# Attention opening of a three-stage kernel: gates of all chunks made together, factor products on another engine, factor set-up in three pieces

## The chip, the cores and the metric

One core of a Trainium2 chip runs the whole program. The metric is the device time of one execution in microseconds. The kernel before took 759.8 us, the median of three runs (759.53 to 760.16).

## What is computed

Three stages follow one another: a gated linear attention with a running state, a mixture of eight experts with one expert for each token, and a dense MLP. The change is in the first. For each batch entry and head it computes, token after token:

```python
m_new = maximum(f_gate[t] + m, i_gate[t])
f_stab = exp(f_gate[t] + m - m_new)
i_stab = exp(i_gate[t] - m_new)
C = f_stab * C + i_stab * outer(v[t], k[t])
n = f_stab * n + i_stab * k[t]
h = C @ q[t]
y[t] = sigmoid(o_gate[t]) * h / maximum(abs(n @ q[t]), 1)
```

There are 4 batch entries, 8 heads, 768 tokens and a head size of 40, all in float32.

## The kernel before

**Tiling.** The 768 tokens are six chunks of 128. A unit is one batch entry of one chunk with all its eight heads; units run chunk by chunk, so units 0 to 3 are chunk 0, units 4 to 7 chunk 1, and there are 24. For a unit, `scores_mm` (L470) multiplies keys with queries (16 products in PSUM), `scan` makes the matrix of decays between the unit's tokens, `scores_w` (L475) weights the scores with it, `pv` (L533) multiplies by the values, `state` (L484) makes the unit's part of the running state, which `state_up` (L501, L505) takes out of PSUM, `inter` (L520) is the part that comes from earlier chunks, and `epilogue1`, `epilogue2` (L545 to L561) and `finish` (L568, L571) normalise. `kweigh` (L461) and `vprime` (L454) weight keys and values on GpSimd. The rows of chunk 0's units are then turned and multiplied with the experts' embeddings (`route_t` L577, `route_l` L608).

**Gates.** The 32 pairs of batch entry and head lie in 32 partitions with the 768 tokens along the row. `fg` and `ig` hold three copies of these rows (96 partitions), loaded by six DMAs (L159): the first copy on SP's queue, the two others on ScalarE's. `gates_m` (L295) is the scan that gives the running maximum, `gates_x` (L300, L301) and `gates_xi` (L305, on VectorE for chunk 0 and on GpSimd for the others) the sums, `gates_exp` (L309) the exponentials. `gates_z` (L315, L316, L318, L319) sets the starts of the scans to zero and, for chunk 0, fills `f0`. `gates_e` (L323) scans the products of the decays.

**Two ways to the decay matrix.** For chunk 0, `scan0` broadcasts the decays of each head to all partitions with products (L445) and scans them on VectorE (L447), twice four heads for each unit. For later chunks the decays go to DRAM (`put_dec`, L276), come back broadcast (`fload`, L285, two DMAs a unit), are scanned over 64 tokens only (L423), and the block between the two halves of the chunk is one product (`far_mm`, L432) of two factors. The early factor `fa` is made by six doublings (`suffix`, L348: widths 63, 62, 60, 56, 48 and 32 for each of five chunks), then `factor_a` (L352, L354) and `spread_a` (L366, four ScalarE operations); the late factor `fb` by `factors` (L359, L361, L362) and `spread_b` (L370, eight ScalarE operations). `gates_pe` (L382 to L389) turns the gates for the later chunks and copies them out of PSUM.

**Order.** The whole attention stands in a manual schedule: each engine runs its instructions in the order of the program text, and each queue its DMAs. Before the loop the order is: loads of unit 0, gates of chunk 0, loads of units 1 and 2, unit 0's scan and scores. In the loop over units: the gates of the later chunks are scanned in unit 0 and finished in unit 1; `gates_z`, `put_dec` and `fload(4)` come in unit 2; the first three doublings in unit 2 and the last three in unit 3; `gates_e` and all of `spread_b` at the end of unit 2; `gates_pe` in unit 3; `factor_a`, `spread_a` and `far_mm(4)` at the end of unit 3. Every unit ends with the loads of the unit three ahead. Set-up that stands outside the manual schedule (constants, `ident_h` L202, masks) is put between by the scheduler.

Of the kernel before, what the change touches and what calls it, by code (L numbers as in the profile page):

```python
# [9 lines left out]
F32 = mybir.dt.float32  # L10
# [4 lines left out]
ALU = mybir.AluOpType  # L15
# [11 lines left out]
def kernel(ctx, tc, qT_in, kT_in, kvo_in, i_gate, f_gate, expert_emb, tau, w12, wio, out, dbg=None):  # L27
# [113 lines left out]
    with ExitStack() as actx:  # L141
# [15 lines left out]
        def load_gates(a, eng):  # L157
            for t, g in ((fg, f_gate), (ig, i_gate)):
                eng.dma_start(out=t[a * BH:(a + 1) * BH], in_=g.rearrange("b h s -> (b h) s"))  # L159

        load_gates(0, nc.sync)
        for a in range(1, 3):
            load_gates(a, nc.scalar)
# [125 lines left out]
        def rows_of(c0, c1, r=None):  # L289
            r = r or slice(0, R3 if c0 else BH)  # L290
            return (lambda t, o=0: t[r, c0 * P + o:c1 * P + o])
# [29 lines left out]
        def gates_e(c0, c1):  # L321
# [3 lines left out]
            n = c1 - c0  # L325
            factors()
            gd = wk.tile([BH, n, B * G], F32, tag="gd", name="gd", bufs=1)
            gd_t[c0] = gd
            nc.vector.tensor_tensor(out=gd, in0=pairm.unsqueeze(1).to_broadcast([BH, n, B * G]),
                                    in1=est[0:BH, c0:c1, P - 1:P].to_broadcast([BH, n, B * G]), op=ALU.mult)  # L330
# [10 lines left out]
        def suffix(second):  # L341

            if not second:
                nc.gpsimd.memset(facA[:, :, HP - 1:HP], 1.0)
                nc.gpsimd.tensor_copy(facA[:, :, 0:HP - 1], fz[:, CH:NCH, 1:HP])
            k = 8 if second else 1
            while k < (HP if second else 8):
                nc.vector.tensor_tensor(out=facA[:, :, 0:HP - k], in0=facA[:, :, 0:HP - k], in1=facA[:, :, k:HP], op=ALU.mult)  # L348
                k *= 2
# [6 lines left out]
        def factors():  # L356
# [5 lines left out]
            nc.vector.tensor_tensor(out=late, in0=late, in1=est[:, CH:NCH, HP - 1:HP].to_broadcast([R3, NCH - CH, HP]), op=ALU.mult)  # L362

# [500 lines left out]
        with tc.manual_schedule():  # L864
# [8 lines left out]
            gates_z(0, 1)  # L873
            nc.sync.dma_start(out=emb, in_=expert_emb)
# [12 lines left out]
            gates_pe0()  # L887
            scores_w(0)
# [3 lines left out]
            for u in range(0, NU - 1):  # L892
# [4 lines left out]
                if ok(u + 2) and u != 2:  # L897
                    fload(u + 2)
# [8 lines left out]
                if u == 1:  # L907
# [3 lines left out]
                    gates_x(1, NCH)  # L911
                    gates_xi(1, NCH)
                    gates_exp(fg, 1, NCH)
                    gates_exp(ig, 1, NCH)
                if u in (2, 3):
                    scores_w(u)
                if u == 2:
# [789 lines left out]
```

## Time and profile before

| | |
|---|---|
| median of three runs | 759.8 us |
| profiled execution | 758.68 us |
| its span on the core | 757.0 us |
| granted TensorE clock, mean | 0.987 |
| busy: TensorE, VectorE, ScalarE, GpSimd | 719.1, 518.7, 370.5, 228.0 us |
| attention units | to about 182 us of the span |

A span starts with the first instruction on the core; the execution's own time has 1.7 us more around it. PE is TensorE's products, PEld its weight loads, DVE VectorE, ACT ScalarE, POOL GpSimd, SP the engine whose queue issues most loads; a q behind the name is the engine's queue. PEclk is the granted clock, 1.00 for 2.4 GHz and 0.50 for 1.2 GHz. In a timeline a row stands for instructions merged (x3: three), with the start, the length, and in brackets how long the engine had been idle before it and what ended that.

### The profile page before, as it was taken

To read this page: it belongs to the slowest core of one execution; us is meant where nothing else is said; L and a number is where in the kernel's file an instruction comes from. 1 tells how busy PE (TensorE), PEld (TensorE's weight loads), DVE (VectorE), ACT (ScalarE), POOL (GpSimd) and SP (SyncE) were. 2 spreads that over 40 slices of the span, in tenths; PEclk is the share of its full clock that TensorE was granted. 3 is DMA by queue.
4 is the path that set the end of the run, shared out by engine and by line. 5 is a ranking of instruction groups with operands and counts; after the bars stand their busy time and mean duration, and the time that the engine had idled before them with its cause. 6 is when DMAs were issued, how large, how long until landed. Compare 5 with 4: busy or idle time off the path is not lost.

```text
span 757.0 us, 13429 instructions
## 1 busy us (share of the span) xinstructions
PE 719.1 (95%) x4773; PEld 674.9 (89%) x4773; DVE 518.7 (69%) x1090; ACT 370.5 (49%) x857; POOL 228.0 (30%) x349
## 2 busy tenths in 40 slices
PE   7679999998889999999999999999999999999995
PEld 7669988998788999999998888998889988899994
DVE  7957879897399989899976764544544554445542
ACT  4375455544466666676645443333333343334442
POOL 5434467785243333454401003003003003002011
PEclk9969999999999999999999999999999999999998
DMA  7258887772458766877832121201110201101000
GB/s 213 83 175 271 273 262 231 215 227 74 148 206 238 237 192 194 227 212 229 250 84 80 27 58 45 57 17 42 37 42 35 42 22 36 43 0 46 12 19 18
DMA packets 70106, 93.14 MB, mean 123 GB/s; under 512 B 31858, under 2 KB 56530, under 8 KB 70034
## 3 DMA queue, kind: packets, MB, share of 16 engines
q1 hardware_dynamic: 66770, 83.96, 38.2%
q0 software_dynamic: 3072, 7.89, 3.0%
q8 instruction: 38, 0.62, 0.3%
q10 hardware_dynamic: 192, 0.39, 0.2%
q14 instruction: 34, 0.28, 0.1%
HBM read 71.11 MB, written 17.18 MB: 117 GB/s over the span
## 4 chain that ended last, share of the span: by engine, by line
issue 42%; PE 23%; POOL 5%; DVE 2%; DMA 1%; ACT 0%; POOLq 0%; SPq 0%; ACTq 0%
PE acc L1207 12%; PE hp L138 10%; POOL out_dram L1252 3%; POOL xr L1358 2%; PE xt L1131 1%; DMA xr<-y 1%; DVE w L121 0%; POOL gap L1254 0%; DVE hs L1181 0%; DVE xl L1133 0%; DVE w L111 0%; DVE fr L1276 0%; POOLq L1702 0%; DVE xl L1149 0%; ACT hs L1520 0%
## 5 line engine op out<-in xcount | busy, mean ns | idle before, releaser
L1207 PE MATMUL acc<-wout,hhl 128*128 128x320 f32 x1152 | 187.0, 309 | 0.0
L1207 PEld LDWEIGHTS acc<-wout,hhl 128*128 128x128 f32 x1152 | 175.9, 188 | 7.4
L1192 DVE TENSOR_TENSOR sg<-hp,sg 128x512 f32<-128x512 f32 (+1 forms) x112 | 68.8, 614 | 93.3 <-ACT sg L1191 86.9
L138 PE MATMUL hp<-xh,win 128*128 128x512 f32 (+1 forms) x560 | 131.0, 364 | 0.0
L1191 ACT ACTIVATE sg<-hp 128x512 f32<-128x512 f32 (+1 forms) x112 | 60.3, 539 | 124.8 <-PE hp L138 124.2
L1194 DVE TENSOR_TENSOR hhl<-sg,hhl 128x512 fp32r<-128x512 f32 (+1 forms) x112 | 71.3, 636 | 70.2 <-ACT hhl L1193 70.2
L1252 POOL DMA_INDIRECT out_dram<-o,tokd x24 | 24.0, 1000 | 312.2 <-ACT o L1236 308.5
L1207 PE MATMUL acc<-w,hs 128*128 128x320 f32 x636 | 104.7, 310 | 2.0 <-ACT hs L1180 1.0
L138 PEld LDWEIGHTS hp<-xh,win 128*128 128x128 f32 x560 | 93.9, 188 | 11.5 <-ACT xh L1397 0.2
L1193 ACT CAST hhl<-sg 128x512 fp32r<-128x512 f32 (+1 forms) x112 | 62.6, 559 | 80.0 <-DVE sg L1192 76.5
L1207 PEld LDWEIGHTS acc<-w,hs 128*128 128x128 f32 x636 | 96.8, 188 | 4.2 <-DVE hs L1181 1.7
L138 PE MATMUL hp<-xl,win 128*128 128x512 f32 (+1 forms) x336 | 85.7, 363 | 0.0
L110 POOL TENSOR_TENSOR w<-r,w 128x256 fp32r<-128x256 f32 x58 | 47.3, 817 | 106.5 <-ACT w L105 83.9
L138 PEld LDWEIGHTS hp<-xl,win 128*128 128x128 f32 x336 | 58.8, 189 | 10.9 <-DVE xl L1398 0.2
L138 PE MATMUL hp<-xh,w 128*128 128x440 f32 (+6 forms) x320 | 66.8, 338 | 0.0
L138 PEld LDWEIGHTS hp<-xh,w 128*128 128x128 f32 x320 | 51.4, 189 | 1.7
L1180 ACT ACTIVATE hs<-hp 128x440 fp32r<-128x440 f32 (+6 forms) x64 | 30.2, 472 | 42.2 <-PE hp L138 38.0
L470 PE MATMUL sp<-qT,kblk 120*128 120x128 f32 x384 | 48.4, 281 | 1.3 <-DVE wm L475 1.3
L470 PEld LDWEIGHTS sp<-qT,kblk 120*128 120x128 f32 x384 | 46.5, 197 | 2.0 <-DVE wm L475 1.4
L533 PE MATMUL op<-vp_in,wm 128*128 128x96 f32 (+1 forms) x368 | 43.6, 272 | 0.0
L533 PEld LDWEIGHTS op<-vp_in,wm 128*128 128x128 f32 x368 | 42.9, 192 | 0.0
L138 PE MATMUL hp<-xl,w 128*128 128x440 f32 (+6 forms) x192 | 42.9, 331 | 0.0
(325 smaller groups left out, 1129.6 us busy)
## 6 DMA issues: line engine op xcount, KB each, us to landing
r<-in_w_dram SPq DMA_DIRECT2D x32, 704.0 KB
kvo<-in_kvo_dram SPq DMA_DIRECT2D x24, 480.0 KB
c<-in_wio_dram SPq DMA_DIRECT2D x16, 704.0 KB
fb<-dec SPq DMA_DIRECT2D x40, 128.0 KB
rows<-zt SPq DMA_DIRECT2D x8, 640.0 KB
qT<-in_qT_dram SPq DMA_DIRECT2D x24, 180.0 KB
xr<-y SPq DMA_DIRECT2D x5, 640.0 KB
kblk<-in_kT_dram SPq DMA_DIRECT2D x48, 60.0 KB
```

The lines of the kernel that those rows point to most:

```text
L110: eng.tensor_tensor(out=t[:, 3 * P:5 * P].rearrange("p (c f) -> p c f", c=2), in0=r1[:, 0:2], in1=hif[:, 0:2], op=ALU.subtract)
L138: nc.tensor.matmul(hp, a, b, start=(i == 0), stop=(i == len(seq) - 1))
L470: nc.tensor.matmul(sp[:, h - hs.start], kblk[u % NLD][0:KR, h // 3, h % 3, :], qT[u][0:KR, h // 3, :], start=True, stop=True)
L533: nc.tensor.matmul(ops[:, h * NW:h * NW + n], wm[u][:, h], vp_in[u % NLD][:, h * DV:h * DV + n], start=True, stop=True)
L1180: nc.scalar.activation(out=hh, in_=hp, func=AF.Relu)
L1191: nc.scalar.activation(out=sg, in_=hp, func=AF.Sigmoid, scale=1.702)
L1192: nc.vector.tensor_tensor(out=g, in0=hp, in1=sg, op=ALU.mult)
L1193: nc.scalar.copy(hh, g)
L1194: nc.vector.tensor_tensor(out=hl, in0=g, in1=hh.bitcast(F32), op=ALU.subtract)
L1207: nc.tensor.matmul(acc_t[blk][i], hl if j == 2 else hh, w[:, DM:2 * DM] if j == 1 else w[:, 0:DM], start=(first and j == 0), stop=(last an ...
L1252: sc = nc.gpsimd.indirect_dma_start(out=out, out_offset=bass.IndirectOffsetOnAxis(ap=tokd[:, ti:ti + 1], axis=0), in_=o[:, i], in_offset=None)
L1358: eng.tensor_tensor(out=xr_t[blk], in0=xr_t[blk], in1=gated[:, t0:t0 + n].unsqueeze(2).to_broadcast([P, n, 3 * P]), op=ALU.mult)
```

## The change

The scan, sums and exponentials of chunks 1 to 5 and the masks move ahead of unit 0's first scan; the scan of chunk 0 now takes all 96 rows at once, and the six gate loads are issued gate by gate instead of copy by copy. `gates_z`, `put_dec` and the decay loads of units 4 and 5 move ahead of unit 0's weighting, and so ahead of the loads of unit 3 on SP's queue. All six doublings go to GpSimd at the end of unit 0, with `gates_e` on VectorE; the late factors (`factor_b`) and half of `spread_b` come at the end of unit 1, `gates_pe` in unit 2, the other half of `spread_b`, `factor_a` and `spread_a` at the end of unit 2, and `far_mm(4)` at its common place in unit 3.

```diff
-        load_gates(0, nc.sync)
-        for a in range(1, 3):
-            load_gates(a, nc.scalar)
+        for t, g in ((fg, f_gate), (ig, i_gate)):
+            nc.sync.dma_start(out=t[0:BH], in_=g.rearrange("b h s -> (b h) s"))
+            for a in range(1, 3):
+                nc.scalar.dma_start(out=t[a * BH:(a + 1) * BH], in_=g.rearrange("b h s -> (b h) s"))
...
-            r = r or slice(0, R3 if c0 else BH)
+            r = r or slice(0, R3)
...
-            factors()
-            gd = wk.tile([BH, n, B * G], F32, tag="gd", name="gd", bufs=1)
...
-        def suffix(second):
-
-            if not second:
-                nc.gpsimd.memset(facA[:, :, HP - 1:HP], 1.0)
-                nc.gpsimd.tensor_copy(facA[:, :, 0:HP - 1], fz[:, CH:NCH, 1:HP])
-            k = 8 if second else 1
-            while k < (HP if second else 8):
-                nc.vector.tensor_tensor(out=facA[:, :, 0:HP - k], in0=facA[:, :, 0:HP - k], in1=facA[:, :, k:HP], op=ALU.mult)
+        def suffix():
+
+            nc.gpsimd.memset(facA[:, :, HP - 1:HP], 1.0)
+            nc.gpsimd.tensor_copy(facA[:, :, 0:HP - 1], fz[:, CH:NCH, 1:HP])
+            k = 1
+            while k < HP:
+                nc.gpsimd.tensor_tensor(out=facA[:, :, 0:HP - k], in0=facA[:, :, 0:HP - k], in1=facA[:, :, k:HP], op=ALU.mult)
                 k *= 2
...
-        def factors():
+        def factor_b():
...
             nc.vector.tensor_tensor(out=late, in0=late, in1=est[:, CH:NCH, HP - 1:HP].to_broadcast([R3, NCH - CH, HP]), op=ALU.mult)
+            n = NCH - CH
+            gd = wk.tile([BH, n, B * G], F32, tag="gd", name="gd", bufs=1)
...
             gates_z(0, 1)
+            gates_m(1, NCH)
+            gates_x(1, NCH)
+            gates_xi(1, NCH)
+            gates_exp(fg, 1, NCH)
+            gates_exp(ig, 1, NCH)
+            masks()
             nc.sync.dma_start(out=emb, in_=expert_emb)
...
             gates_pe0()
+            gates_z(1, NCH)
+            put_dec()
+            fload(4)
+            fload(5)
             scores_w(0)
...
-                if ok(u + 2) and u != 2:
+                if ok(u + 2) and u > 3:
                     fload(u + 2)
...
-                    gates_x(1, NCH)
-                    gates_xi(1, NCH)
-                    gates_exp(fg, 1, NCH)
-                    gates_exp(ig, 1, NCH)
...
-                if u == 2:
-                    gates_z(1, NCH)
-                    put_dec()
-                    fload(4)
...
-                    for a in range(1, 3):
-                        gates_m(0, 1, slice(a * BH, (a + 1) * BH))
-                    gates_m(1, NCH)
-                    masks()
...
-                if u in (2, 3):
-                    suffix(u == 3)
-                if u == 3:
+                if u == 2:
                     gates_pe(1, NCH)
...
-                if ok(u + 1) and u != 3:
+                if ok(u + 1):
                     far_mm(u + 1)
...
+                if u == 0:
+                    suffix()
+                    gates_e(1, NCH)
+                if u == 1:
+                    factor_b()
+                    spread_b(0, H // 2)
                 if u == 2:
-                    gates_e(1, NCH)
-                    spread_b(0, H)
-                if u == 3:
+                    spread_b(H // 2, H)
                     factor_a()
                     spread_a()
-                    far_mm(4)
```

## Rows read from the trace of the kernel before

**Rows 1.** Table of stretches: busy us of each engine, PEclk, DMA share, GB/s
```profile
20.00:33.00 13.00, 10.56 (x92) 10.07 (x92) 12.76 (x20) 4.83 (x11) 5.14 (x8) 1.00 0.18 55
33.00:52.00 19.00, 10.67 (x57) 9.35 (x56) 12.59 (x18) 11.98 (x33) 6.89 (x12) 0.64 0.64 201
52.00:70.00 18.00, 18.00 (x163) 17.72 (x163) 11.48 (x30) 10.63 (x35) 9.61 (x19) 1.00 0.68 206
...
230.00:757.00 527.00, 517.56 (x3133) 483.17 (x3131) 337.81 (x622) 250.85 (x517) 104.56 (x149) 0.99 0.32 91
```

**Rows 2.** Timeline of TensorE (start us, us, what, idle before)
```profile
7.04 3.78 PE L445 MATMUL f<-f,ident 128*128 128x128 f32 x16 [1.70 <-DVE f L319]
...
38.95 0.31 PE L383 MATMUL pg<-ident,fd 32*128 32x32 f32 x1 [4.78 <-DVE fd L362]
...
48.94 3.28 PE L470 MATMUL sp<-qT,kblk 120*128 120x128 f32 x16
...
56.26 1.95 PE L470 MATMUL sp<-qT,kblk 120*128 120x128 f32 x16
```

**Rows 3.** Timeline of VectorE
```profile
4.67 0.41 DVE L295 TENSOR_TENSOR_SCAN mm<-fg,ig 32x128 f32<-32x128 f32 x1 [0.89 <-DMA ig<-in_i_gate_dram]
...
18.57 0.86 DVE L295 TENSOR_TENSOR_SCAN mm<-fg,ig 32x128 f32<-32x128 f32 x2
...
22.45 1.32 DVE L300 TENSOR_TENSOR fg<-fg,mm 96x640 f32<-96x640 f32 x1
23.81 0.82 DVE L301 TENSOR_TENSOR fg<-fg,mm 96x640 f32<-96x640 f32 x1
...
32.61 2.75 DVE L348 TENSOR_TENSOR mm<-mm 96x315 f32<-96x315 f32 x3
35.28 2.08 DVE L323 TENSOR_TENSOR_SCAN fd<-fg,fd 96x640 f32<-96x640 f32 x1
37.89 0.48 DVE L361 TENSOR_TENSOR fb<-fd,fb 32x320 fp32r<-32x320 f32 x1 [0.53 <-ACT fb L359]
...
40.20 1.21 DVE L423 TENSOR_TENSOR_SCAN tri<-fb,id 128x512 f32<-128x512 f32 x1
43.71 0.17 DVE L557 SCALAR_TENSOR_TENSOR dn<-num 128x8 f32<-128x8 f32 x1 [2.30 <-ACT num L554]
...
44.24 2.56 DVE L348 TENSOR_TENSOR mm<-mm 96x280 f32<-96x280 f32 x3
...
52.33 1.22 DVE L475 TENSOR_TENSOR wm<-sp,pmb 128x1024 f32<-128x1024 f32 x1 [3.26 <-PE sp L470]
```

**Rows 4.** Timeline of the DMA issues and of ScalarE in the first 10 us
```profile
4.59 0.35 ACTq L159 DMA_DIRECT2D ig<-in_i_gate_dram  x1
...
5.91 0.29 SPq L874 DMA_DIRECT2D emb<-in_emb_dram  x1
...
9.39 0.47 ACT L404 ACTIVATE emb_sq<-emb 8x320 f32<-8x320 f32 x1 [3.14 <-DMA emb<-in_emb_dram]
```

**Rows 5.** Waits of SP's queue, 0 to 200 us (us in total, times, longest)
```profile
SPq L285 <- DMA dec<-fg: 2.4, 1, 2.4
```

**Rows 6.** Timeline of GpSimd
```profile
21.10 1.31 POOL L305 TENSOR_TENSOR ig<-ig,mm 96x640 f32<-96x640 f32 x1 [2.98 <-DVE mm L295]
22.38 0.72 POOL L454 TENSOR_TENSOR vp_in<-kvo,ei_tok 128x320 f32<-128x320 f32 x1
```

**Rows 7.** VectorE's groups by line and form, 0 to 60 us
```profile
L447 DVE TENSOR_TENSOR_SCAN pmb<-f,ident_h 128x512 f32<-128x512 f32 x8 | 9.4, 1209 | 1.5 <-PE f L445 1.5
```

**Rows 8.** Timeline of ScalarE
```profile
26.46 1.28 ACT L539 ACT_TABLE_LOAD   x1
...
38.41 3.73 ACT L370 ACTIVATE rhsB<-fb,hmask 96x320 fp32r<-96x320 f32 x8 [0.55 <-DVE fb L361]
...
47.84 1.92 ACT L366 ACTIVATE lhsA<-fa,bmask 96x320 fp32r<-96x320 f32 x4 [0.55 <-DVE fa L354]
```

**Rows 9.** Decay loads of SP's queue (ns min/median/max of one issue, first and last start)
```profile
L285 SPq DMA_DIRECT2D fb<-dec x40: 302/582/1857, 32.1 to 162.8; - x40
```

More of the change, by code (lines that the diff above doesn't have):

```diff
@@ L155 @@
         fg = ap1.tile([R3, S], F32, name="fg")
-        def load_gates(a, eng):
-            for t, g in ((fg, f_gate), (ig, i_gate)):
-                eng.dma_start(out=t[a * BH:(a + 1) * BH], in_=g.rearrange("b h s -> (b h) s"))
-        load_gates(0, nc.sync)
-        for a in range(1, 3):
-            load_gates(a, nc.scalar)
+        for t, g in ((fg, f_gate), (ig, i_gate)):
+            nc.sync.dma_start(out=t[0:BH], in_=g.rearrange("b h s -> (b h) s"))
+            for a in range(1, 3):
+                nc.scalar.dma_start(out=t[a * BH:(a + 1) * BH], in_=g.rearrange("b h s -> (b h) s"))
         NLD = 3
@@ L324, in gates_e @@
                                          op0=ALU.mult, op1=ALU.add)
-            n = c1 - c0
-            factors()
-            gd = wk.tile([BH, n, B * G], F32, tag="gd", name="gd", bufs=1)
-            gd_t[c0] = gd
-            nc.vector.tensor_tensor(out=gd, in0=pairm.unsqueeze(1).to_broadcast([BH, n, B * G]),
-                                    in1=est[0:BH, c0:c1, P - 1:P].to_broadcast([BH, n, B * G]), op=ALU.mult)
         def masks():
@@ L362, in factors @@
             nc.vector.tensor_tensor(out=late, in0=late, in1=est[:, CH:NCH, HP - 1:HP].to_broadcast([R3, NCH - CH, HP]), op=ALU.mult)
+            n = NCH - CH
+            gd = wk.tile([BH, n, B * G], F32, tag="gd", name="gd", bufs=1)
+            gd_t[CH] = gd
+            nc.vector.tensor_tensor(out=gd, in0=pairm.unsqueeze(1).to_broadcast([BH, n, B * G]),
+                                    in1=est[0:BH, CH:NCH, P - 1:P].to_broadcast([BH, n, B * G]), op=ALU.mult)
         def spread_a():
```

## The prediction, made before the changed kernel was run

> **What bounds the kernel now.** I read the table of stretches first, then TensorE's order of time, then those of VectorE, GpSimd and ScalarE, and last the queues. From 230 us on TensorE is busy 517.56 of 527 us, and from 52 to 70 us all 18.00 of 18 [rows 1]: there the products are the bound, and neither DMA nor another engine can win anything. The opening is different. From 20 to 33 us VectorE is busy 12.76 of 13 us and TensorE 10.56; from 33 to 52 us TensorE has only 10.67 of 19 us and its granted clock averages 0.64 [rows 1]. So the opening is set by VectorE, then by ScalarE and VectorE in turn, and TensorE pays twice. It stands idle 4.78 us until the late factors are made (L362), and after that it runs at the lower of its two levels, 1.2 instead of 2.4 GHz: the scores of unit 4 take 3.28 us for 16 products, those of unit 5 take 1.95 [rows 2]. What the change saves before unit 4 is weighted should stay saved, as all behind it is one train of products whose loads are issued unit by unit.
>
> **Where the end is measured.** I follow VectorE, because its list is fixed and nearly full, to the weighting of unit 4's scores (L475), which starts at 52.33 us [rows 3]. Two points lie on the way: the start of the first gate scan (4.67) and the end of unit 4's scan (40.20 + 1.21 = 41.41) [rows 3].
>
> **Part 1, the first gates wait for six loads.** Until now the first scan works on 32 rows and waits for SP's two loads. It will work on 96 rows, at the same length per row, so its own time stays, but it needs the loads on ScalarE's queue too, and the last of them goes out at 4.59 us [rows 4]; the new order of the loads leaves that one last. When it lands no row shows. Lower end: no later than SP's own, so the scan stays at 4.67. Upper end: the small embedding load is issued at 5.91 and its reader starts at 9.39, 3.48 us on [rows 4], which gives 8.07. The write of the decays is waited for 2.4 us past its issue of 0.35 or so, as that of ScalarE's load here [rows 4, 5], which gives 7.3. I take 7.7, between the last two: **+3.0 us**.
>
> **Part 2, moved gate work.** The scan over chunks 1 to 5, its two sums (1.32 and 0.82 us [rows 3]), GpSimd's subtraction (1.31 [rows 6]) and the two masks go ahead of unit 0's first scan. VectorE pays the same there as it paid later, so the chain only changes order. What lies behind them gets later (unit 0's scan, and all of unit 0), what lay behind them gets earlier. Two gains come with it: the two extra short scans for rows 32 to 95 go (**-0.86** [rows 3]), and VectorE's waits for the broadcast products, 1.5 us in eight scans [rows 7], are filled by the moved work (**-1.5**). The set-up from ident_h on stands behind the first gates now; I leave it there. ScalarE's exponentials all come before its other functions, so a return to their table goes, and with it the reload of the sigmoid's, 1.28 us [rows 8]; ScalarE has idle time around it, so I count nothing. Without that idle time it would be a gain of 1.28 for each.
>
> **Part 3, the doublings go to GpSimd.** VectorE loses 2.75 us before unit 4's scan and 2.56 us after it [rows 3]. GpSimd's two-input operations cost 0.72 us at 320 elements and 1.31 at 640 [rows 6], or 1.8 ns an element: widths 315, 310, 300, 280, 240 and 160 make about 3.8 us. They start behind unit 1's weighted keys; behind them wait v' and weighted keys of unit 2, which the products of unit 2 need a good 8 us later, and ScalarE's cast of the early factors, later still. So they lie beside other work: **-2.75** in the first stretch, nothing added. Without that cover every further us would come back as a us.
>
> **Part 4, ports.** While GpSimd made a v' of 0.72 us from 22.38 on, the 96x640 sum on VectorE (from 22.45) took 1.32 us, and its twin behind it 0.82 [rows 3, 6]: the loss is 0.5 us. The decay scan (2.08 [rows 3]) already had a GpSimd operation beside it and keeps its price. The Trainium skill (SBUF — State Buffer, Who interferes with whom) says that a VectorE operation with two SBUF inputs and a GpSimd operation that reads SBUF exclude each other, the later one blocking for the whole of the other; that speaks against this change, and the pair above agrees with it in kind. By the rule taken to its end the sum would be 2.6 us instead of 6.4, as a rival below has it.
>
> **Part 5, the factors in pieces.** The subtraction that ends the early factors (L354) moves ahead of unit 4's scan. Its price is 0.48 us, that of the same operation on the late ones (L361 [rows 3]); before it stands a wait for ScalarE's cast, which follows half of the head spreads (half of 3.73 [rows 8]). That wait lies between nothing and 1.9; I take 0.7 as ScalarE starts the half early: **+1.2** together. To the end of unit 4's scan: 41.41 + 3.0 - 0.86 - 1.5 - 2.75 + 1.2 = **40.5 us**.
>
> **Part 6, from there to unit 4's weighting** took 10.92 us before: 2.30 of wait for a copy that stood behind the spreads on ScalarE, the three doublings 2.56, unit 5's scan, a wait of 3.26 for slow scores, the rest small operations [rows 3]. Now ScalarE has half of the head spreads, a cast and the four batch spreads (1.92 [rows 8]) in front of unit 2's state copy, and this copy, the copy of unit 4's scan and that of unit 2's sums follow it. Walking these in order gives VectorE waits of 1.5 (sums), 1.6 (routing logits) and 0.4 (scores), with 1.2 for unit 5's scan and 0.7 of small work: **5.4 us**. That puts the weighting at 45.9 instead of 52.33: **6.4 us** earlier. In this walk TensorE's longest pause is 2.5 us, so I keep the full clock and the scores at 1.95.
>
> **Part 7, SP's queue.** The write of the decays and two units' decay loads now stand before the loads of unit 3. SP waits for the gates (about 18 us), 2.4 us for the write, and issues four loads at 0.58 [rows 9]: unit 3's loads start near 23 us and, with 3.48 to land, are there by about 29; its scores are due near 34. Counted as nothing; every us of lateness beyond 5 would cost one.
>
> **The sum.** The profiled execution took 758.68 us with a span of 757.0, the median of the three runs is 759.8, or 1.1 more. 758.68 - 6.4 = 752.3 there, and 759.8 - 6.4 = **753.4 us** against the median.
>
> **The rivals.**
> A. The sixth load lands with the first two, or nearly. For it: its queue had nothing else to do. Against: the issue at 4.59. It gives back 3.0: 750.4, and 749.2 if the waits of 0.7 (part 5) and 0.5 (part 4) do not come. Chance 0.16.
> B. The clock falls again in unit 3's pause, since 2.5 us idle, little work and 1.4 us idle follow each other. For it: 4.78 us of pause ended at half clock [rows 2]. The price is 3.28 - 1.95 = 1.33 for the scores and 0.8 for what surrounds them: 755.5. Chance 0.13.
> C. GpSimd's doublings shut VectorE out one by one, 3.8 us: 757.2. For it the pair of sums; against it, most of VectorE's work beside them reads PSUM, whose scans keep a mean of 1.21 us [rows 7]. Chance 0.04.
> D. The gain is made and lost again behind unit 4, or the lead is never there: 759.8, 0.05. Loads by unit and a full TensorE speak against it.
> E. Slower: TensorE starts cold and stays at the lower level. The pause before the broadcast products grows from 1.70 to 4.7 us, and they took 3.78 us for 16 even before [rows 2]. If the level stayed low through the work that now fills 20 to 33 us, its 10.56 us of products would take 21.1, 8.1 more than that stretch: the 6.4 lost and 1.7 on top, 761.5. It decides once more than some 8 us of products run at half speed beyond what VectorE covers. Against it: from 20 to 33 us the clock holds 1.00 although TensorE works only 10.56 of 13 us [rows 1]. Chance 0.06.
>
> **The numbers.** The forecast has 0.56. A measurement here can tell 0.2% (1.5 us) from no change. Faster: forecast, A, B and C, 0.89; same: D, 0.05; slower: E, 0.06. The range runs from A's 749.2 to C's 757.2, and leaves out D, E and little more.
>
> **What would show it.** Right: the first gate scan near 7.7 us; no idle TensorE before the gate transposes; six GpSimd products of 0.4 to 0.9 us by about 28 us; unit 4's weighting near 46; granted clock 1.00 from 33 to 52. Wrong: a gate scan past 10, a clock of 0.5 about the scores of unit 4, GpSimd operations over 1.5 us, or a pause of VectorE on a decay load.

## The result and the profile after

The changed kernel takes **752.12 us**, median of four runs (751.23 to 752.44), against 759.98 for the kernel before in the same comparison: a ratio of 0.9894, 95% interval 0.9877 to 0.9911. The prediction was 753.4. The profiled execution took 751.84 us with a span of 750.1 (before 758.68 and 757.0), so 6.8 us less. (With a fourth run, made beside the changed kernel's, the median of the kernel before is 759.98 instead of 759.8. In the ratios further down, four slow executions of 769 to 1432 us are left out: two of the kernel before, one of experiment 1 and one of experiment 7.)

The table of stretches of the changed kernel, against [rows 1]:

```profile
20.00:33.00 13.00, 11.99 (x109) 11.52 (x107) 12.73 (x19) 4.34 (x14) 8.62 (x12) 1.00 0.67 204
33.00:52.00 19.00, 17.37 (x137) 16.71 (x138) 12.48 (x23) 14.01 (x45) 13.07 (x24) 0.91 0.62 194
52.00:70.00 18.00, 17.15 (x157) 16.62 (x157) 13.42 (x38) 10.98 (x34) 8.74 (x11) 1.00 0.86 267
230.00:750.00 520.00, 510.69 (x3091) 476.68 (x3089) 330.90 (x609) 246.65 (x508) 100.93 (x144) 0.99 0.32 88
```

From 33 to 52 us TensorE went from 10.67 to 17.37 busy us, and its mean clock from 0.64 to 0.91: the pause and most of the half speed are gone. From 230 us on it is as full as before.

TensorE's timeline after, against [rows 2] (L440 is L445 of before, L465 is L470, L378 is L383):

```profile
10.32 3.39 PE L440 MATMUL f<-f,ident 128*128 128x128 f32 x16 [4.98 <-DVE f L316]
...
31.43 0.24 PE L378 MATMUL pg<-ident,fd 32*128 32x32 f32 x1 [0.36 <-DVE fd L352]
...
33.71 1.42 PE L479 MATMUL dC<-vp_in,kw 128*120 128x123 f32 x6 [1.30 <-ACT Cst L496]
34.92 3.01 PE L465 MATMUL sp<-qT,kblk 120*128 120x128 f32 x16
...
43.17 1.95 PE L465 MATMUL sp<-qT,kblk 120*128 120x128 f32 x16
...
49.16 1.95 PE L465 MATMUL sp<-qT,kblk 120*128 120x128 f32 x16
```

The pause of 4.78 us ahead of the gate transposes is 0.36 now. Up to unit 5 the clock still falls once, at unit 3: its scores take 3.01 us. Those of units 4 and 5 run at full speed, and unit 5's start at 49.16 instead of 56.26, 7.1 us earlier.

VectorE's timeline after, against [rows 3] (L292 is L295, L298 is L301, L320 is L323, L351 is L361, L344 is L354, L418 is L423, L470 is L475), and then GpSimd's, against [rows 6]:

```profile
8.04 0.42 DVE L292 TENSOR_TENSOR_SCAN mm<-fg,ig 96x128 f32<-96x128 f32 x1 [4.26 <-DMA kvo<-in_kvo_dram]
...
10.20 1.53 DVE L292 TENSOR_TENSOR_SCAN mm<-fg,mm,ig 96x640 f32<-96x640 f32 x1
...
12.62 1.82 DVE L298 TENSOR_TENSOR fg<-fg,mm 96x640 f32<-96x640 f32 x1
...
14.77 2.32 DVE L442 TENSOR_TENSOR_SCAN pmb<-f,ident_h 128x512 f32<-128x512 f32 x2
...
22.68 1.47 DVE L320 TENSOR_TENSOR_SCAN fd<-fg,fd 96x640 f32<-96x640 f32 x1
...
28.34 2.52 DVE L351 TENSOR_TENSOR fb<-fd,fb 32x320 fp32r<-32x320 f32 x1
...
36.60 1.12 DVE L344 TENSOR_TENSOR fa<-mm,fa 32x320 fp32r<-32x320 f32 x1 [0.52 <-ACT fa L342]
37.97 1.23 DVE L470 TENSOR_TENSOR wm<-sp,pmb 128x1024 f32<-128x1024 f32 x1 [0.24 <-PE sp L465]
39.11 1.22 DVE L418 TENSOR_TENSOR_SCAN tri<-fb,id 128x512 f32<-128x512 f32 x1
...
45.23 1.23 DVE L470 TENSOR_TENSOR wm<-sp,pmb 128x1024 f32<-128x1024 f32 x1 [0.52 <-PE sp L465]
```

```profile
22.66 5.79 POOL L338 TENSOR_TENSOR mm<-mm 96x315 f32<-96x315 f32 x6
28.42 0.72 POOL L449 TENSOR_TENSOR vp_in<-kvo,ei_tok 128x320 f32<-128x320 f32 x1
29.10 0.73 POOL L456 TENSOR_TENSOR kw<-kvo,pmb 128x320 f32<-128x320 f32 x1
29.80 0.72 POOL L449 TENSOR_TENSOR vp_in<-kvo,ei_tok 128x320 f32<-128x320 f32 x1
```

Read the two together. The late factors' subtraction (L351) starts at 28.34 and needs 0.48 us [rows 3], but ends at 30.86, after the last of three GpSimd operations that follow one another from 28.42 to 30.52. It waited for no data: its inputs, the decay scan and ScalarE's cast, had ended at 24.15 and 25.93. VectorE counts as busy all that time; here a blocked operation shows as a long one, not as a wait. Unit 4's scan (L418) ends at 40.33, and unit 4 is weighted (the last L470) at 45.23.

### The profile page after: what moved, and what is told of

Its sections match the earlier page's. It is cut to its first block, busy times and chain, and to the rows that moved or that the text cites. A ratio compares the mean times of both kernels' runs of the same rounds, so it can differ in the third digit from the quotient of the medians.

```text
span 750.1 us, 13424 instructions
## 1 busy us (share of the span) xinstructions
PE 717.7 (96%) x4773; PEld 673.9 (90%) x4773; DVE 513.7 (68%) x1082; ACT 367.9 (49%) x855; POOL 235.9 (31%) x355
## 4 chain that ended last, share of the span: by engine, by line
issue 42%; PE 23%; POOL 5%; DVE 2%; DMA 1%; ACT 0%; POOLq 0%; SPq 0%; ACTq 0%
PE acc L1201 12%; PE hp L138 10%; POOL out_dram L1246 3%; POOL xr L1352 2%; PE xt L1125 1%; DMA xr<-y 1%; DVE w L121 0%; POOL gap L1248 0%; DVE hs L1175 0%; DVE xl L1127 0%; DVE w L111 0%; DVE fr L1270 0%; POOLq L1696 0%; DVE xl L1143 0%; ACT hs L1514 0%
## 5 line engine op out<-in xcount | busy, mean ns | idle before, releaser
L1201 PE MATMUL acc<-wout,hhl 128*128 128x320 f32 x1152 | 187.0, 309 | 0.0
L1201 PEld LDWEIGHTS acc<-wout,hhl 128*128 128x128 f32 x1152 | 175.9, 188 | 7.4
L1201 PE MATMUL acc<-w,hs 128*128 128x320 f32 x636 | 104.9, 310 | 2.0 <-ACT hs L1174 1.0
L1201 PEld LDWEIGHTS acc<-w,hs 128*128 128x128 f32 x636 | 96.8, 188 | 4.5 <-DVE hs L1175 1.9
L465 PE MATMUL sp<-qT,kblk 120*128 120x128 f32 x384 | 48.4, 280 | 0.2 <-DVE wm L470 0.2
L465 PEld LDWEIGHTS sp<-qT,kblk 120*128 120x128 f32 x384 | 46.3, 197 | 1.1 <-DVE wm L470 0.6
```

Source lines behind the costliest of these rows:

```text
L465: nc.tensor.matmul(sp[:, h - hs.start], kblk[u % NLD][0:KR, h // 3, h % 3, :], qT[u][0:KR, h // 3, :], start=True, stop=True)
L1201: nc.tensor.matmul(acc_t[blk][i], hl if j == 2 else hh, w[:, DM:2 * DM] if j == 1 else w[:, 0:DM], start=(first and j == 0), stop=(last an ...
```

## The experiments

All start from the changed kernel unless said otherwise. The table has the points of the path that each one moves: start of the first gate scan, weighting of unit 4, scores of unit 5, first product of an expert's output (L1201, L1207 before), in us of the profiled execution; then its span and the ratio of the timed runs to the kernel before, run beside it.

| kernel | gate scan | weighting 4 | scores 5 | expert | span | ratio, 95% interval |
|---|---|---|---|---|---|---|
| before | 4.67 | 52.33 | 56.26 | 197.47 | 757.0 | 1 |
| changed | 8.04 | 45.23 | 49.16 | 190.34 | 750.1 | 0.9894 (0.9877 to 0.9911) |
| 1 doublings on VectorE | 7.33 | 46.89 | 50.83 | 195.98 | 755.6 | 0.9940 (0.9906 to 0.9974) |
| 2 doublings later | 7.65 | 45.62 | 49.56 | 189.84 | 749.4 | 0.9920 (0.9896 to 0.9943) |
| 3 sixth load on SP | 5.86 | 44.83 | 48.76 | 186.52 | 746.1 | 0.9913 (0.9882 to 0.9945) |
| 4 spare products, unit 2 | 7.36 | 46.15 | 50.09 | 189.97 | 749.5 | 0.9909 (0.9881 to 0.9938) |
| 5 no doublings | 7.22 | 42.52 | 46.45 | 186.18 | 745.7 | 0.9891 (0.9862 to 0.9919) |
| 6 before, doublings on GpSimd | 4.68 | 48.91 | 53.30 | 194.10 | 753.9 | 0.9960 (0.9933 to 0.9987) |
| 7 as 3, spare products, unit 3 | 6.08 | 43.55 | 47.48 | 188.18 | 747.7 | 0.9898 (0.9849 to 0.9947) |
| 8 first gates on 32 rows | 4.20 | 43.93 | 47.87 | 188.26 | 747.8 | 0.9901 (0.9862 to 0.9939) |
| 9 doublings first | 6.77 | 42.92 | 46.86 | 191.63 | 751.2 | 0.9913 (0.9888 to 0.9938) |
| 10 = 7 and 9 | 6.35 | 43.38 | 47.32 | 189.23 | 748.8 | 0.9875 (0.9851 to 0.9899) |
| 11 factors at their old places | 7.38 | 49.90 | 53.84 | 195.22 | 754.8 | 0.9962 (0.9942 to 0.9981) |
| 12 = 10, spare products at 163 us | 5.95 | 42.97 | 46.91 | 185.95 | 746.1 | 0.9868 (0.9841 to 0.9895) |

Span less expert column is 559.5 to 560.2 in every row: behind that point nothing moves. All columns but the last are of one profiled execution, and the executions of one kernel differ by 1 to 9 us: that of experiment 1 took 757.3 us where the median of its runs is 754, and those of 3, 5 and 9 were the fastest of theirs. So a column shows where time went in that execution, and only the ratio says what a kernel is worth. The intervals of most experiments overlap that of the changed kernel; those of 6 and 11 stand clear of it, and that of 1 overlaps by 0.0005.

The seven kernels with the changed kernel's opening start their first scan anywhere from 6.77 to 8.04, so a difference under 1 us at unit 5 shows nothing. From unit 5's scores to the experts it took 141.21 us before and 141.18 after, but 137.8 to 145.2 in the others; of that below.

**1. Doublings back on VectorE**, at their new place.

```diff
-                nc.gpsimd.tensor_tensor(out=facA[:, :, 0:HP - k], ...
+                nc.vector.tensor_tensor(out=facA[:, :, 0:HP - k], ...
```

> The changed kernel with its six doublings back on VectorE, at the place they now have at the end of unit 0. Two theories. Port theory: VectorE and GpSimd operations with their inputs in SBUF exclude each other, so much of what VectorE saved came back as blocking (the factor subtraction at 28.34 us took 2.52 us where its like took 0.48). Then VectorE pays some 2.5 us for six undisturbed doublings and gets 0.6 to 2 us of blocking back: scores of unit 5 start at 49.7 to 51.1 us (49.16 in the changed kernel), time 752.6 to 754. Rival, the sum of the prediction: the doublings cost VectorE the 5.3 us they cost in the kernel before and nothing comes back: scores of unit 5 near 54.5, time near 757.4.

VectorE and TensorE:

```profile
22.66 2.76 DVE L338 TENSOR_TENSOR mm<-mm 96x315 f32<-96x315 f32 x6
...
30.73 0.68 DVE L351 TENSOR_TENSOR fb<-fd,fb 32x320 fp32r<-32x320 f32 x1
```

```profile
28.00 3.56 PE L465 MATMUL sp<-qT,kblk 120*128 120x128 f32 x16 [3.44 <-DVE wm L470]
```

Six doublings cost VectorE 2.76 us here, and the subtraction is back to 0.68. Unit 5's scores come 1.67 us later than in the changed kernel, at 50.83, though the gates started 0.71 earlier: inside the range of the port theory and far from the rival's 54.5. So moving the doublings is worth 1.7 to 2.4 us in the opening, less than VectorE is spared. A pause of 3.44 us and scores at half clock (3.56 us) are part of that; they now stand at unit 2. At this place the doublings cost VectorE half of the 5.31 they took before [rows 3], where GpSimd worked beside them (from 31.69 to 36.02 and from 44.08 to 46.61). The expert column is not typical of this kernel: in the profiled execution the clock fell twice more, to means of 0.83 from 120 to 130 us and 0.86 from 140 to 150.

**2. Doublings one unit later**, behind unit 2's weighted keys.

```diff
                 if u == 0:
-                    suffix()
                     gates_e(1, NCH)
                 if u == 1:
+                    suffix()
                     factor_b()
```

> The changed kernel with the doublings still on GpSimd, but one unit later, behind the weighted keys of unit 2, so that GpSimd is not in arrears when VectorE reaches the factor subtraction. Port theory: the subtraction falls from 2.52 us to 0.5 to 1.2, scores of unit 5 start at 47.2 to 48.2 us, time about 750.5 to 751. Rival: the stretch is set by ScalarE's spreads and the cast of the early factors, which now wait longer: scores of unit 5 at 48.9 to 50, no gain or a loss.

VectorE:

```profile
27.92 0.69 DVE L351 TENSOR_TENSOR fb<-fd,fb 32x320 fp32r<-32x320 f32 x1
...
33.21 2.49 DVE L552 SCALAR_TENSOR_TENSOR dn<-num 128x8 f32<-128x8 f32 x1
```

The subtraction is short again, and another operation is blocked in its place: one of 8 elements a partition takes 2.49 us, where others of its kind take 0.14. The blocking follows GpSimd's train. Nothing is won at unit 5: the port theory's 47.2 to 48.2 failed. The rival's range was met, but not by its mechanism, for the early factors did not wait longer: unit 4's scan starts at 38.09, 1.02 earlier than in the changed kernel. That lead is lost behind it, where unit 4's scores take 2.54 us after a pause of 2.50.

**3. The sixth gate load on SP's queue.**

```diff
-                nc.scalar.dma_start(out=t[a * BH:(a + 1) * BH], ...
+                (nc.sync if t is ig and a == 2 else nc.scalar).dma_start(out=t[a * BH:(a + 1) * BH], ...
```

> The changed kernel with the last of the six gate loads on SP's queue, third there, instead of fourth on ScalarE's, where it goes out only at 4.33 us. Theory: the late issue alone makes the first gate scan wait (8.04 us); issued at about 1.7 it lands by 5 to 5.7, the scan starts there, and all behind it moves by 2.3 to 3: scores of unit 5 at 46.2 to 46.9, time 749.2 to 750. Rival: the transfers share full DMA engines, the load lands at 7 or later and the gain is under 1 us; or the lead is lost in the waits of units 2 and 3 (gate scan early, scores of unit 5 still near 49).

The first scan starts 2.18 us earlier. At unit 5's scores 0.40 is left of it: the theory's 46.2 to 46.9 failed, and the second rival held (a lead lost in the waits of units 2 and 3). TensorE:

```profile
38.62 0.83 PE L479 MATMUL dC<-vp_in,kw 128*120 128x123 f32 x6 [2.08 <-ACT Cst L496]
...
41.92 2.80 PE L465 MATMUL sp<-qT,kblk 120*128 120x128 f32 x16
```

Unit 3's scores kept the full clock (1.99 us), but behind the next pause, 2.08 us, the clock fell under unit 4's, which took 2.80. That is the prediction's rival B at its place.

**4. Spare products behind the gate transposes of unit 2**, so that TensorE doesn't stand idle ahead of unit 3's scores.

```diff
                 if u == 2:
                     gates_pe(1, NCH)
+                    keep_warm(ps_1.tile([P, H, NI], F32, tag="ip", ...), 12)
```

> The changed kernel with twelve idle products on TensorE behind the gate transposes of unit 2, where it pauses 1.3 us before the clock falls. If the fall costs what the slow scores show (3.01 us against 2.05), the granted clock stays 1.00 from 30 to 40 us, and unit 5's scores start 1 us earlier, near 48.2. Rival: the fall is covered, since VectorE waits only 0.24 us for the slow scores of unit 3: unit 5's scores move by 0.3 us at most although the clock stays up.

TensorE:

```profile
31.68 2.94 PE L84 MATMUL ipw<-ident 128*128 128x128 f32 x24
35.03 1.99 PE L465 MATMUL sp<-qT,kblk 120*128 120x128 f32 x16
42.75 3.29 PE L465 MATMUL sp<-qT,kblk 120*128 120x128 f32 x16
```

(The 12 calls show as 24 products.) Unit 3's scores are at full speed and most of unit 4's at half: the fall went on to behind the next pause, of 0.74 us. Unit 5's scores come 0.93 later than in the changed kernel; neither expectation, 1 us earlier or within 0.3, held.

**5. No doublings at all**: the loop of `suffix` is left out, so the early factors lack their products.

```diff
-            k = 1
+            k = HP
             while k < HP:
```

> The changed kernel without its six doublings: the early factors are left wrong, every other operation stays, and GpSimd is free where they stood. If the two engines shut each other out of SBUF there, the early-late subtraction (2.52 us in the changed kernel) takes at most 1.2 us, ScalarE's first half of the head spreads starts 1.3 to 2.5 us earlier than 30.89, and the scores of unit 5 start 1 to 2 us earlier than 49.16. If instead the place of the doublings costs nothing because ScalarE's order sets the pace of units 2 and 3, the scores of unit 5 stay within 0.6 us of 49.16. If the clock falls at units 3 or 4 as before, some of the lead goes into scores that take 2.5 to 3.3 us instead of 1.95.

The subtraction took 0.69 us, unit 5's scores came at 46.45, 2.71 earlier, with units 3 and 4 at full clock. Its gates started 0.82 earlier, which unit 0's scan keeps (13.95 for 14.77); the other **1.9 us** are what GpSimd's doublings still cost the opening of the changed kernel, by blocking and by what the slow clock at unit 3 adds. It is a figure of the opening in one profile each: the ratio of the timed runs is 0.9891 against 0.9894, so they show no gain.

**6. The kernel before with its doublings on GpSimd**, at their old places.

```diff
-                nc.vector.tensor_tensor(out=facA[:, :, 0:HP - k], ...
+                nc.gpsimd.tensor_tensor(out=facA[:, :, 0:HP - k], ...
```

> The kernel before with one part of the change alone: its six doublings go to GpSimd at their old places. By the prediction's own sum this part gives 2.75 us up to unit 4's scan; if that is the part that carries the change, unit 4's weighting comes 2 to 4 us earlier than 52.33 and the time falls by 2 to 4 us. If the two engines shut each other out, the second three doublings and the subtraction of the late factors just take turns, and the weighting comes less than 1 us earlier. If the gain lies in the order of the factors and not in their engine, the time stays within 1 us of the kernel before.

Unit 4's weighting came 3.42 us earlier, the span fell by 3.1 and the ratio agrees (0.4% of 759 us is 3.0). So the first expectation held (2 to 4 us). In the opening the part is worth less than these profiles say: this one was 0.67 us ahead before its first doubling (the scan of unit 2 starts at 23.88 instead of 24.55). This part alone carries less than half of the change.

**7. The earlier load and spare products in unit 3's pause.**

```diff
                 if rts:
                     route_t(rts[0])
+                if u == 3:
+                    keep_warm(ps_1.tile([P, H, NI], F32, tag="ip", ...), 12)
```

> The changed kernel with its sixth gate load on SP's queue, and with 24 spare products in unit 3's pause of TensorE, between the transposes of unit 0's output and the state products of unit 3. If a pause at unit 3 is what takes the clock from unit 4's scores, these scores take 1.95 to 2.05 us instead of 2.80, unit 4's weighting starts at 43.5 to 44.2 and the scores of unit 5 at 47.2 to 47.9, and the time is 0.5 to 1.5 us below that of the earlier load alone. If the fall goes on to the next pause (unit 4, or unit 5), the scores of unit 5 stay at 48.3 to 49.2 and the time stays within 0.5 us of it.

TensorE:

```profile
32.70 1.99 PE L465 MATMUL sp<-qT,kblk 120*128 120x128 f32 x16
...
41.49 1.95 PE L465 MATMUL sp<-qT,kblk 120*128 120x128 f32 x16
```

and VectorE:

```profile
56.62 1.23 DVE L418 TENSOR_TENSOR_SCAN tri<-fb,id 128x512 f32<-128x512 f32 x1 [1.60 <-DMA fb<-dec]
```

No fall in the opening any more, and unit 5's scores 1.28 us ahead of experiment 3, as expected. The span of the profiled execution is 1.6 longer all the same. Further on TensorE's pauses up to 143 us are 1.6 longer in sum (6.6 for 5.1), and VectorE waits 4.2 us for decay loads (1.6 in 3), 1.60 of it ahead of unit 7's scan, the line above. The rest lies in the handover to the experts, where the clock fell from 165 to 170 us (0.68) and did not in 3. The timed ratios, 0.9898 and 0.9913, do not tell the two apart.

**8. The first gates on 32 rows again**, with the two short scans ahead of the long one.

```diff
-            r = r or slice(0, R3)
+            r = r or slice(0, R3 if c0 else BH)
...
+            for a in range(1, 3):
+                gates_m(0, 1, slice(a * BH, (a + 1) * BH))
             gates_m(1, NCH)
```

> The changed kernel with the first gates on 32 rows again, so that the first scan waits for SP's two loads only, and with two short scans for the other 64 rows ahead of the scan over chunks 1 to 5. The first scan starts near 4.7 us instead of 7.4 to 8.0. By the prediction's sum the change paid 3.0 - 0.86 = 2.1 us here: if the first gates set the opening, unit 5's scores come 1.5 to 2.2 us earlier than 49.16. If the six loads bind in any case, since the scan over chunks 1 to 5 needs all of them and now stands ahead of unit 0's scan, the short scans come on top and unit 5's scores come 0 to 1 us later.

VectorE:

```profile
4.20 0.41 DVE L292 TENSOR_TENSOR_SCAN mm<-fg,ig 32x128 f32<-32x128 f32 x1 [0.43 <-DMA ig<-in_i_gate_dram]
...
7.00 0.86 DVE L292 TENSOR_TENSOR_SCAN mm<-fg,ig 32x128 f32<-32x128 f32 x2
7.90 1.55 DVE L292 TENSOR_TENSOR_SCAN mm<-fg,mm,ig 96x640 f32<-96x640 f32 x1
...
13.49 2.31 DVE L442 TENSOR_TENSOR_SCAN pmb<-f,ident_h 128x512 f32<-128x512 f32 x2
```

Neither expectation held: unit 0's scan starts 1.28 us earlier than in the changed kernel and unit 5's scores 1.29. Of the 3.84 us by which the first scan starts earlier, 1.54 are gone at the long scan (the two short ones, and a copy into `f0` of 1.24 instead of 0.21) and 1.02 between that and unit 0's scan, where the set-up now stands. In the other kernels with the changed opening unit 0's scan starts at 13.50 to 14.77, so the price of the joint scan, with the two short scans set against it, is between 0 and 1.3. In the timed runs it does not show (0.9901 and 0.9894).

**9. Doublings first**: ahead of unit 1's v' in GpSimd's order.

```diff
             gates_z(1, NCH)
+            suffix()
             put_dec()
...
                 if u == 0:
-                    suffix()
                     gates_e(1, NCH)
```

> The changed kernel with its six doublings ahead of unit 1's v' in GpSimd's order, right behind the gates' reset marks, so that they run from about 16.5 us, where GpSimd stood idle, and are through by about 21. Port theory: what leaving the doublings out gave, or most of it, comes back with them in place: the late factors' subtraction takes at most 1.2 us instead of 2.52, unit 4's weighting starts at 42.3 to 43.8 instead of 45.23, the scores of unit 5 at 46.2 to 47.7 instead of 49.16, and the span is 1 to 3 us below 750.1. Rival: the blocking only moves again, as it did when the doublings stood later: some other VectorE operation beside them (unit 0's v', the scans of unit 1) takes 1.5 us more than it did, and the scores of unit 5 start at 48.5 or later.

VectorE, and the table of stretches:

```profile
27.59 0.94 DVE L351 TENSOR_TENSOR fb<-fd,fb 32x320 fp32r<-32x320 f32 x1
...
42.92 1.23 DVE L470 TENSOR_TENSOR wm<-sp,pmb 128x1024 f32<-128x1024 f32 x1 [0.52 <-PE sp L465]
...
92.04 1.43 DVE L418 TENSOR_TENSOR_SCAN tri<-fb,id 128x512 f32<-128x512 f32 x1 [1.61 <-DMA fb<-dec]
```

```profile
185.00:190.00 5.00, 4.07 (x22) 4.07 (x23) 2.84 (x21) 2.79 (x9) 2.71 (x4) 0.66 0.25 73
```

The opening came out as the port theory said: a subtraction of 0.94 us and the weighting at 42.92, 2.31 earlier. But 1.27 of that is an earlier start of unit 0's scan (13.50 for 14.77), so about 1.0 is the gain of the new place; VectorE now waits 1.69 us for ScalarE's cast ahead of the early subtraction (0.52 in the changed kernel). The span did not follow: it is 1.1 longer than the changed kernel's, and the timed ratio is no better either (0.9913 for 0.9894). Of the lead of 2.30 at unit 5's scores, 1.7 goes in longer pauses of TensorE up to 143 us (7.1 in sum, 5.4 in the changed kernel; half a us of it behind the late decay load above, which the changed kernel waits 1.43 for), and the rest and more goes in the handover to the experts, where the clock fell at 185 us.

**10. All three together**: the edits of 3, 7 and 9.

> The doublings ahead of unit 1's v', the sixth gate load on SP's queue, and 24 spare products in unit 3's pause of TensorE. If the three places are separate losses on one path, the gains add: the earlier load 1.0 to 2.0 us on top of the doublings' place, scores of units 3 and 4 at 1.95 to 2.05 us, unit 5's scores at 44.5 to 46.3, and a time 4 to 6 us below the changed kernel's where no other pause takes the clock. If ScalarE (head and batch spreads) is the next bound, unit 5's scores start no earlier than 46.0 whatever comes before it.

VectorE:

```profile
34.81 1.07 DVE L344 TENSOR_TENSOR fa<-mm,fa 32x320 fp32r<-32x320 f32 x1 [1.89 <-ACT fa L342]
```

The gains do not add. VectorE waits 1.89 us for ScalarE's cast ahead of the early subtraction, as it did in 9 (1.69). That cast stands behind the second half of the head spreads (32.51 to 34.43), which ScalarE starts only after its copies of the gate transposes, so the order there is the likely next bound; no run changes it. Unit 5's scores start at 47.32, no earlier than in experiment 9: the sum's 44.5 to 46.3 failed, and the rival's bound of 46.0 held.

**11. The factors at their old places**, gates still ahead, doublings on GpSimd.

```diff
-                if ok(u + 1):
+                if ok(u + 1) and u != 3:
                     far_mm(u + 1)
...
-                if u == 0:
-                    suffix()
+                if u == 2:
                     gates_e(1, NCH)
-                if u == 1:
                     factor_b()
-                    spread_b(0, H // 2)
-                if u == 2:
-                    spread_b(H // 2, H)
+                    spread_b(0, H)
+                if u == 3:
                     factor_a()
                     spread_a()
+                    far_mm(4)
```

(`suffix()`, with all six doublings, stands behind unit 1's sums in unit 2, where the kernel before had the first three, and `gates_pe` in unit 3, as before.)

> The changed kernel with its factors where the kernel before had them: decay scan, late factors and all eight head spreads at the end of unit 2, early factors, batch spreads and the far products of unit 4 at the end of unit 3, the doublings on GpSimd behind unit 1's sums. The gates stay ahead of the first unit. If the spreading over three units carries the gain, unit 4's weighting comes at 48 to 50.5 us and the time is 3 to 5 us above the changed kernel's. If the gates made ahead carry it (with the doublings on GpSimd, which alone gave 3.0), unit 4's weighting stays below 46.5 and the time within 1 us of the changed kernel's. If the gates ahead cost more than they give, the weighting comes after 48.91, where it was with the doublings alone.

VectorE:

```profile
31.40 3.63 DVE L320 TENSOR_TENSOR_SCAN fd<-fg,fd 96x640 f32<-96x640 f32 x1
...
49.90 1.23 DVE L470 TENSOR_TENSOR wm<-sp,pmb 128x1024 f32<-128x1024 f32 x1 [3.35 <-PE sp L465]
```

The weighting falls back to 49.90: the pause and the half clock are there again (scores of unit 4: 3.37 us), and the decay scan, which then runs beside GpSimd, takes 3.63 instead of 1.47. Together with 6 this divides the 7.10 us at unit 5's scores: doublings alone 56.26 - 53.30 = 2.96; gates ahead on top of that 53.30 - 53.84 = **-0.54**; the spreading over three units, with the doublings' place that goes with it, 53.84 - 49.16 = **4.68**. The timed ratios, 0.9960 for 6, 0.9962 for 11 and 0.9894, divide the time in the same way: about 3, 0 and 5 us. The middle step is not the gates alone. The decay scan took 1.84 us in 6, so the step holds 1.8 us of blocking from the new place of the doublings; and the 0.67 us by which 6 was ahead before its first doubling count in the first step and against the middle one. What is shown is that the gates made ahead, with the factors at their old places, gained no time that these runs can tell; they had to be early for the spreading.

**12. Spare products where the attention hands over to the experts**, on top of 10.

```diff
                 if u == NU - 2:
+                    keep_warm(ps_1.tile([P, H, NI], F32, tag="ip", ...), 7)
                     inter(u + 1, True)
```

> The three together, and 14 spare products (about 1.7 us) in the pause of TensorE near 163 us, where the attention hands over to the experts: ahead of the last unit's products of the state, which wait 1.60 us there, and behind which the clock was 0.66 from 165 to 170. If the leads of the opening are given back there by the clock, the granted clock stays at 1.00 from 160 to 180, the first product that adds up expert sums starts 1.5 to 3 us earlier than 189.23, and the span is 745.5 to 747.5 instead of 748.8. If the fall only moves on to the next pause (near 180 or 186 us), as it did from unit 3 to unit 4, that first product starts at 188.3 or later and the span stays above 748.

The same five microseconds in the tables of the changed kernel, of 10 and of 12:

```profile
165.00:170.00 5.00, 4.07 (x22) 3.98 (x23) 2.61 (x10) 2.66 (x9) 2.56 (x5) 0.68 0.18 66
```

```profile
165.00:170.00 5.00, 5.00 (x31) 4.91 (x31) 2.58 (x13) 1.47 (x5) 2.92 (x5) 0.66 0.25 88
```

```profile
165.00:170.00 5.00, 5.00 (x47) 5.00 (x45) 3.91 (x14) 1.29 (x4) 3.10 (x5) 1.00 0.19 69
```

The clock held at 1.00 from 160 to 190, the experts began 3.28 us earlier than in 10 (0.41 of it stood at unit 5's scores already), and the span of the profiled execution is 2.7 shorter, about as the first expectation had it. The timed ratios, 0.9868 and 0.9875, do not separate the two. By its ratio this is the fastest of the kernels; it beats the kernel before, and its interval still overlaps the changed kernel's.

## Why the prediction was right, and which of its terms were not

**The path was the right one.** VectorE to unit 4's weighting was predicted at 45.9 and came at 45.23; the end of unit 4's scan at 40.5, and came at 40.33. The lead was carried to the experts one for one (7.10 at unit 5's scores, 7.13 there). The sum was 6.4, the profiled executions differ by 6.84, the median is 1.3 us below the forecast. That it came so close is in part luck. In the sum errors of over 3 us met, as the parts below show. And the prediction took it that what is saved before unit 4 stays saved, as all behind is one train of products; the experiments gain or lose up to 4 us there (137.8 to 145.2), and the two kernels compared happened to take the same 141.2. Of its signs of being right, the clock of 1.00 from 33 to 52 us failed (0.91); of its signs of being wrong, one came, GpSimd operations over 1.5 us (the first doubling took 2.00 beside the decay scan, and the subtraction of the gates 1.95).

**Part 1**, the first scan at 7.7: it came at 8.04, and at 6.77 to 7.65 in six other kernels with this opening. The start was sized well. That all of it delays what follows was not: with the two short scans set against it the forecast is 3.0 - 0.86 = 2.1, and the price was at most 1.3 (experiment 8).

**Part 2.** The two short scans (0.86) and the 1.5 us of waits for broadcast products [rows 7] went as forecast. The set-up did not stay behind the first gates: it fills the gaps between the small gate operations, and from the first scan to the next one it is 2.16 us, where the kernel before needed 3.42 to the wait ahead of its unit 0's scan. Part of that was two longer copies beside GpSimd. VectorE of the kernel before, and then GpSimd:

```profile
6.20 0.79 DVE L319 COPY f<-fg 32x128 f32<-32x128 f32 x1
6.34 0.92 DVE L202 COPY ident_h<-ident 128x512 f32<-128x512 f32 x1
...
9.15 1.22 DVE L447 TENSOR_TENSOR_SCAN pmb<-f,ident_h 128x512 f32<-128x512 f32 x1 [1.06 <-PE f L445]
...
12.68 1.22 DVE L475 TENSOR_TENSOR wm<-sp,pmb 128x1024 f32<-128x1024 f32 x1 [0.59 <-PE sp L470]
...
14.38 0.69 DVE L455 COPY vp_in<-ei_tok 128x8 f32<-128x8 f32 x1
```

```profile
6.18 0.73 POOL L264 MEMSET fd<- 96x768 f32 x1
...
14.20 0.84 POOL L454 TENSOR_TENSOR vp_in<-kvo,ei_tok 128x320 f32<-128x320 f32 x1
```

The three copies end 0.03 to 0.35 us after GpSimd's fill and its v'. In the changed kernel they stand beside neither and take 0.21, 0.42 and 0.16. Two waits that the sum did not count went too: 0.59 us ahead of the weighting of unit 0, and 0.53 ahead of the late subtraction [rows 3].

**Part 3**, -2.75: VectorE was spared that much, as forecast; experiment 1 shows 2.76 for all six at the new place. The term for GpSimd was too small, six products in 5.79 us instead of 3.8; 4.62 with little beside them (experiment 2). "Nothing added" was wrong, as part 4 shows.

**Part 4**, contention, is **the mis-sized term**. The sum kept the 0.5 us inside the price of the moved gate sums and added nothing. The second sum of the gates took 1.82 for 0.82, the late subtraction 2.52 for 0.48, the early one 1.12 for 0.48: 3.7 us. Against it the first sum lost its 0.5, the decay scan fell from 2.08 to 1.47, for it had not been unhindered before either, and the three copies above got 1.6 shorter: about 1.0 net by these lengths, and some 1.6 of VectorE's time, as two of the copies overlap by 0.65 us. So blocking was there before, and moved to other operations. Leaving the doublings out shows 1.9 us to be had in the opening. The rule of the Trainium skill (SBUF — State Buffer, Who interferes with whom) that the later of the two blocks for the whole of the other's instruction holds in kind. In size the trace goes further: L351 waited for the last doubling and three more instructions, as GpSimd's next one each time came before VectorE's turn. That does not always happen. In experiments 1 and 5 the same subtraction began beside the first of two GpSimd instructions and took 0.68 and 0.69, while the second took 0.97 instead of 0.72; what decides it is open. The rule taken to its end as rival C had it, 757.2, is refuted, since most of VectorE's work beside the doublings kept its price (the scans of unit 2: 2.32 for two).

**Part 5**, +1.2 for the early subtraction: 1.12 and a wait of 0.52, 1.6. **Part 6**, 5.4: 45.23 - 40.33 = 4.9. **Part 7**: SP wrote the decays at 17.36, unit 3's loads went out from 21.81 (forecast 23), and nothing waited for them.

**The rivals.** A: the sixth load was not early; brought forward (3), it gave the opening 0.4 us at unit 5, not 3.0. B: the clock did fall once, but under unit 3's scores and not unit 4's, and there VectorE lost only 0.24 us to it. C is answered under part 4. D: not so. E: the broadcast products came after 4.98 us of idle time and from 20 to 33 us the clock was 1.00 nevertheless.

**What stays open.** From unit 5's scores to the experts the same program text takes 137.8 to 145.2 us. What the rows show of it: VectorE's waits for decay loads (in sum 1.6 us in 1 and 3, 2.7 before, 2.4 after, 4.2 in 7), and falls of the clock. In most kernels it falls once in the handover, between 160 and 180 us; in 9 at 185 to 190, in 1 between 120 and 160, and nowhere in the kernel before, 3 and 12. In its profile, experiment 12 kept the clock and the lead; as 3 kept both without spare products there, and the timed ratios of 10 and 12 agree, that holding the clock brings the gain to the end is likely but not shown. Why the clock falls at one place in one kernel and at another in the next is not settled, and so two experiments that won 1.3 and 2.3 us in the opening over their neighbours (7 over 3, 9 over the changed kernel) ended no sooner. The split of the opening's gain between its parts rests on one profile of each kernel; only the coarse split of experiment 11 is borne out by timed runs.

## What to carry to other kernels

Add up a change on the engine whose list is full, from a point that it shifts to the point where another engine takes over; that sum was good to 1 us here while single terms were off by 2, so don't read the terms off a good sum. Before moving work from VectorE to GpSimd, look at which two-input operations of VectorE will stand beside a train of GpSimd operations, and put the train where there are none: in the profile the same six products cost about 1 us less at unit 5 when they stood earlier, in GpSimd's idle time (experiment 9; the timed runs don't show it). A gain in front of a pause of TensorE can be lost if the clock falls on the products behind the pause, so follow the gain up to where nothing moves any more, and let the timed runs decide whether it is one.

## What was not expected of the hardware

A VectorE operation of 8 elements a partition took 2.49 us (0.14 alone), blocked by a train of GpSimd operations and shown as busy. Spare products took the fall of the clock out of one pause and it came at the next one (unit 3's scores from 3.01 to 1.99 us, unit 4's from 1.95 to 3.29); in experiment 3 the scores behind a pause of 2.08 us ran at the lower level, in experiment 9 those behind one of 1.56 us at the same place did not. The length of one pause does not decide it: ahead of unit 3's state products it was 1.30 us in the changed kernel, where the clock fell, and 1.30 in experiment 3, where it did not.
